# A fused attention and mixer kernel: the low-rank U product with x stationary, a turn by one matmul, other PSUM banks and a new order of the small steps

## The chip, the core and the metric

The kernel runs on one core of one Trainium2 chip. The metric is device time in microseconds (us) of one execution; several runs are taken and their median is given. TensorE does matrix products and writes them to PSUM, which has eight banks of 512 fp32 columns in each of 128 partitions. VectorE (DVE in the profile), ScalarE (ACT) and GpSimd (POOL) work on elements; SyncE (SP) issues DMAs. Each engine takes its instructions in the order in which the program gives them, and waits for others through semaphores.

## The reference

The inputs are q, k and v (batch 4, 8 heads, 768 positions, head width 64, fp32), and the mixer's U (768x32), V (32x768), w_ch1 (512x2048) and w_ch2 (2048x512). The output is 4x768x512 in fp32.

```python
def attn(q, k, v, n_global=8, n_local=96):
    scores = q @ k.transpose(0, 1, 3, 2) / sqrt(64)
    # keep: the first 8 positions, and the 96 positions up to and including the own one
    # bias: -slope[h] * distance (n_local for a far global position)
    a = softmax(where(keep, scores + bias, -1e9))
    return a @ v

def mixer(x, U, V, w_ch1, w_ch2):              # x: [batch, seq, 512], heads side by side
    h = x.transpose(0, 2, 1) @ U @ V           # mixes positions through rank 32
    u = x + h.transpose(0, 2, 1)
    return u + maximum(u @ w_ch1, 0) @ w_ch2
```

## The kernel before

**Attention.** Two heads make a pair, and the four batches of four pairs are 16 pairs, numbered `i`. Of the 768 positions, each block of 128 queries sees its own block of keys and the one before, in which 8 columns are replaced by the global keys (`kA`; `vA` for the values). The scores of one head are 1408 columns, made in three chunks `c` = 0, 1, 2 of 512, 512 and 384 columns. `s_pe` makes a chunk on TensorE (lines 361 and 366) in one of two `sc` banks, `s_dve` (line 392) adds the bias on DVE and empties the bank, `st_E` (line 404) takes one exponential over the 1408 columns on ACT. `st_V` (lines 416 and 420) multiplies by the values into the single `ob` bank; DVE takes a reciprocal (line 425) and scales into `x_sb` (line 433), POOL casts to fp16 (`x16`, line 434). Each matmul in `st_V` has 65 columns: 64 values and the sum of the softmax.

**Mixer, first part.** Once both heads of a pair are in `x16` (128 positions x 128 features for each of six blocks), the pair's slice of the low-rank product follows. `st_M1` multiplies U by x: six matmuls with U, padded from 32 to 128 columns, as the stationary operand and x as the moving one (line 442), summed in a bank; DVE copies the result, 128x128 with features along the columns, into `tmp16` (line 446). `st_M3` multiplies V by it, two halves of three matmuls (line 483), each half followed by an addition into `x_sb` on DVE (line 488); POOL casts the sum back to `x16` (line 491), and `st_X` transposes that by a DMA on SP's queue into `uT` (line 471). Batch 0 has another second half, `st_M2`, which the change doesn't touch.

**Mixer, second part.** `queue_ff` puts the large products of a batch's half into two queues: an "up" unit is four matmuls of 384 columns into a bank of the `th` kind (line 506), emptied by ACT with a ReLU into `htr` (line 510); a "down" unit is four matmuls of 512 columns into a `cps` bank (line 526), and after four of them DVE adds `x_sb` (line 532) and SP stores the result. `fill(n)` takes the next n units from these queues. It stands between the small steps, so that TensorE has something to do while other engines prepare the next step.

**PSUM.** Eight banks: two `sc`, one `ob`, two `cps` (down units and a few others) and three `th`. The `th` banks serve the up units, the transposes of q and k (`st_T`) and, before the change, the U product and both halves of `st_M3`.

**Order.** The program's order is written out by hand. After a first part for batch 0 (to about 33 us) a loop runs over `i` = 4 to 17; "step i" below is one turn of it. In step i the scores of pair i are made, the attention output of pair i-1 (`st_V`), and the low-rank product of pair i-1 (`st_M1`, `st_M3`, `st_X`). Pairs up to 7 get their transposes on TensorE (`st_T`), later ones by DMAs (`turn`, lines 324 and 327, on SP's queue), and then the key copies `st_K` (lines 340 and 341, on DVE) and the query copies `st_Z` (line 335, on POOL) prepare pair i+1 in step i. `cast_qk` (line 112) casts q and k of pair i+2 on POOL. `st_P` (line 311) is a small DVE copy into `vA` for pairs below 8. A step takes ten units (13 from step 9 on). Down units are held back until step 7, and in steps 9, 10 and 14 the queue gives up units for a while, as a new half begins there.

The tile `zw` is 128x512 in fp16, set to zero at the start and used only by the warm-up matmuls (`warm`, in the first 18 us).

Of the kernel before, what the change touches and what calls it, by code (L numbers as in the profile page):

```python
# [16 lines left out]
ALU = mybir.AluOpType  # L17
# [3 lines left out]
def kernel(  # L21
# [13 lines left out]
    nc = tc.nc  # L35
# [3 lines left out]
    P = 128  # L39
    DM = H * D  # L40
    NSB = S // P
# [3 lines left out]
    R = moe_U.shape[1]  # L45
    NP = H // 2
    NPE = 2 * NP
# [13 lines left out]
    GT = S // 2  # L61
    NTG = GT // P
# [11 lines left out]
    def ps_sc(tag="sc"):  # L74
        return psum.tile([P, 512], FP32, name="sc", tag=tag, bufs=2)

    def ps_ob():
        return psum.tile([P, 512], FP32, name="ob", tag="ob", bufs=1)
# [4 lines left out]
    def ps_th(name, dtype=FP32, cols=512):  # L83
        return psum.tile([P, cols], dtype, name=name, tag="th", bufs=3)
# [47 lines left out]
    NPAIR = B * NP  # L132
# [20 lines left out]
    zw = cst.tile([P, 512], FP16, name="zw")  # L153
# [27 lines left out]
    u16 = cst.tile([P, NSB, P], FP16, name="u16")  # L181
    v16w = cst.tile([P, S], FP16, name="v16w")
    for t in (qz[1][0][D:P], qz[1][1][0:D], u16.rearrange("p n c -> p (n c)"), v16w):
        nc.gpsimd.memset(t.bitcast(I32), 0)
    ident16 = cst.tile([P, P], FP16, name="ident16")
# [37 lines left out]
    w1v = moe_w_ch1.rearrange("(c p) n -> p c n", p=P)  # L223
    w2v = moe_w_ch2.rearrange("(c p) n -> p c n", p=P)

    def load_w1(c):
        js = slice(c * (DFF // 4), (c + 1) * (DFF // 4))
        nc.gpsimd.dma_start(w1_16[:, :, js], w1v[:, :, js])

    def load_w2(c):  # L230
        nc.gpsimd.dma_start(w2_16[:, 4 * c:4 * c + 4], w2v[:, 4 * c:4 * c + 4])


    xs, x16s, tmps, uTs = {}, {}, {}, {}

    def new_batch(b):
        xs[b] = xp.tile([P, NSB, DM], FP32, name="x_sb", tag="x_sb", bufs=3)
        x16s[b] = xp.tile([P, NP, NSB, P], FP16, name="x16", tag="x16")
        tmps[b] = xp.tile([P, DM], FP16, name="tmp16", tag="tmp16", bufs=3)
        uTs[b] = xp.tile([P, NDC, S], FP16, name="uT", tag="uT")  # L240
# [90 lines left out]
    def st_Z(i):  # L331
        tq = turned.pop(i).rearrange("d n p -> d (n p)")
        for hi in range(2):
            r = slice(hi * D, (hi + 1) * D)
            nc.gpsimd.tensor_copy(qz[i % 2][hi][r], tq[r])  # L335

    def st_K(i):
        kT = kts[i]
        kA = kp.tile([P, NSB - 1, P], FP16, name="kA", tag="kA")
        nc.vector.tensor_copy(kA.rearrange("d n p -> d (n p)"), kT[:, 0:S - P])  # L340
        nc.vector.tensor_copy(
            kA[:, 1:, 0:NG], kT[:, 0:NG].unsqueeze(1).broadcast_to((P, NSB - 2, NG))
        )
        kas[i] = kA
# [53 lines left out]
    def st_S(i, c):  # L398
        for hi in range(2):
            s_dve(i, hi, s_pe(i, hi, c))  # L400

    def st_E(i, hi):
        ep = scp.tile([P, W], FP16, name=f"ep{hi}", tag=f"ep{hi}")
        nc.scalar.activation(  # L404
            ep, sps.pop((i, hi)), AF.Exp, scale=slope[2 * (i % NP) + hi]
        )
        eps[i, hi] = ep
# [29 lines left out]
    def st_M1(i):  # L437
        b, dc = i // NP, i % NP
        ch = slice(dc * P, (dc + 1) * P)
        tps = ps_th("tmp_ps")  # L440
        for n in range(NSB):
            nc.tensor.matmul(  # L442
                tps[:, 0:P], u16[:, n], x16s[b][:, dc, n],
                start=(n == 0), stop=(n == NSB - 1),
            )
        nc.vector.tensor_copy(tmps[b][:, ch], tps[:, 0:P])

    def st_M2(i):
        b, dc = i // NP, i % NP
        ch = slice(dc * P, (dc + 1) * P)  # L450
        for g in range(2):
            ups = ps_th("ups")
            nc.tensor.matmul(
                ups[:, 0:GT], tmps[b][:, ch], v16w[:, g * GT:(g + 1) * GT],
                start=True, stop=False,
            )
            for t in range(NTG):
                nc.tensor.matmul(
                    ups[:, t * P:(t + 1) * P], x16s[b][:, dc, NTG * g + t], ident16,
                    start=False, stop=(t == NTG - 1),  # L460
                )
            dst = uTs[b][:, dc, g * GT:(g + 1) * GT]
            if dc < NP - 2 or (g == 0 and dc == NP - 1):
                nc.vector.tensor_copy(dst, ups[:, 0:GT])
            else:
                nc.scalar.copy(dst, ups[:, 0:GT])


    def st_X(i):
        b, dc = i // NP, i % NP  # L470
        nc.sync.dma_start_transpose(
            uTs[b][:, dc].rearrange("d (n p) -> d n p", n=NSB),
            x16s[b][:, dc].rearrange("p n d -> p (n d)"),
        )

    def st_M3(i):
        b, dc = i // NP, i % NP
        ch = slice(dc * P, (dc + 1) * P)
        for g in range(2):
            ups = ps_th("ups")  # L480
            for t in range(NTG):
                n = NTG * g + t
                nc.tensor.matmul(  # L483
                    ups[:, t * P:(t + 1) * P], v16w[:, n * P:(n + 1) * P], tmps[b][:, ch],
                    start=(t == 0), stop=(t == NTG - 1),
                )
            dst = xs[b][:, NTG * g:NTG * (g + 1), ch]
            nc.vector.tensor_tensor(  # L488
                dst, ups[:, 0:GT].rearrange("p (t d) -> p t d", t=NTG), dst, ALU.add
            )  # L490
        nc.gpsimd.tensor_copy(x16s[b][:, dc], xs[b][:, :, ch])  # L491

    ups_q, downs_q = deque(), deque()

# [70 lines left out]
    def fill(n):  # L565
        for _ in range(n):
            down = downs_q and not held[0] and not any(w == downs_q[0][1] for _, w in ups_q)
            room = ups_q and (not downs_q or downs_q[0][1] == ups_q[0][1]
                              or ups_q[0][1] in follows(downs_q[0][1]))
            if down and room:  # L570
                if ahead[0] > 0:
                    ahead[0] -= 4
                    downs_q.popleft()[0]()
                else:
                    ahead[0] += 3
                    ups_q.popleft()[0]()
            elif down:
                downs_q.popleft()[0]()
            elif room:
                ups_q.popleft()[0]()  # L580
            else:
                return

    def follows(w):
        b, g = w
        return ((b, 1),) if g == 0 else ((b + 1, 0),)
# [8 lines left out]
    for i in range(NP):  # L595
# [7 lines left out]
        if i == 2:  # L603
            load_w1(0)
        if i == 3:
            load_v(NP)
            load_w1(2)
        if i >= 2:
            st_M1(i - 2)
# [15 lines left out]
        if i == 2:  # L625
            load_w1(1)
# [19 lines left out]
    for i in range(NP, NPAIR + 2):  # L646
        b, hp = divmod(i, NP)
        live = i < NPAIR
        n = 1 if i < 2 * NP + 1 else 2
        held[0] = i < NP + 3  # L650
        if hp == 0 and live and b + 1 < B:
            new_batch(b + 1)
        if live and i > NP:
            st_S(i, 0)
        early = {NP: (NP + 2,), NP + 1: (NP + 3,), NP + 2: (NP + 5,)}
        for j in early.get(i, (i + 3,)):
            if j < NPAIR:
                load_qk(j)
        if i + 1 < NPAIR:
            load_v(i + 1)  # L660
        if i == NP + 1:
            load_qk(NP + 4)
        fill(2)
        if NP < i <= NPAIR:
            st_V(i - 1, 0)
        if i + 1 < NPE:
            st_T(i + 1)
        if live:
            cast_v(i)
            st_A(i)  # L670
            if i == NP + 1:
                load_w2(2)
        fill(n)
        if live:
            st_S(i, 1)
        fill(1)
        if NP < i <= NPAIR:
            st_V(i - 1, 1)
        if i == NP + 1:
            load_w2(3)  # L680
        if i > NP + 1 and (i - 2) % NP == NP - 1:
            queue_ff((i - 2) // NP, 0)
            queue_ff((i - 2) // NP, 1)
            ahead[0] = 1
        if i == NPAIR + 1:
            break
        fill(n)
        if live:
            st_S(i, 2)
            if i < NPE:  # L690
                st_P(i)
        if i + 1 < NPAIR:
            if i + 1 >= NPE:
                st_K(i + 1)
                st_Z(i + 1)
        if i + 2 < NPAIR:
            cast_qk(i + 2, nc.gpsimd)
        if i == NP:
            load_w2(0)
            load_w2(1)  # L700
        fill(1)
        if i > NP:
            st_M1(i - 1)
        if live:
            st_E(i, 0)
        fill(2)
        if i > NP:
            st_M3(i - 1)
            st_X(i - 1)
        if live:  # L710
            st_E(i, 1)
        if i + 2 < NPAIR and i + 2 >= NPE:
            turn(i + 2)
        fill(1 + n)
    while ups_q or downs_q:
        fill(1)
    ordered.close()
# [35 lines left out]
```

## Time and profile before

| | |
|---|---|
| median of 3 runs | 245.12 us (244.91 to 245.6) |
| the profiled execution's own time | 244.88 us |
| its span in the profile | 243.1 us |
| TensorE (PE) busy | 230.5 us, 95% |
| weight loads (PEld) | 141.4 us, 58% |
| DVE, ACT, POOL busy | 132.6, 118.8 and 93.8 us |
| line 442, U product | 96 matmuls of 128 columns, 16 of the groups of six |
| line 483, V product | 72 matmuls of 128 columns, 12 groups of six |

The profile is of one execution on the chip. An engine's busy time is the union of its instructions' spans. Matmuls are pipelined: the span of one (219 ns for 128 columns) is longer than the time after which the next can start (56 ns), so that TensorE reads as busy where it loses a little. The page gives shares of the span, a chain of waits followed back from the last instruction, and the groups of instructions by line. The timeline lists instructions with start, duration, engine and line, out<-in and a count; neighbours of one line are merged. A wait is given in brackets with the engine and line that ended it. Names as `hps<-uT,w` are the tiles written and read.

### The profile page before, as it was taken

To read this page: it belongs to the slowest core of one execution; us is meant where nothing else is said; L and a number is where in the kernel's file an instruction comes from. 1 tells how busy PE (TensorE), PEld (TensorE's weight loads), DVE (VectorE), ACT (ScalarE), POOL (GpSimd) and SP (SyncE) were. 2 spreads that over 40 slices of the span, in tenths; PEclk is the share of its full clock that TensorE was granted. 3 is DMA by queue.
4 is the path that set the end of the run, shared out by engine and by line. 5 is a ranking of instruction groups with operands and counts; after the bars stand their busy time and mean duration, and the time that the engine had idled before them with its cause. 6 is when DMAs were issued, how large, how long until landed. Compare 5 with 4: busy or idle time off the path is not lost.

```text
span 243.1 us, 4884 instructions
## 1 busy us (share of the span) xinstructions
PE 230.5 (95%) x1952; PEld 141.4 (58%) x1952; DVE 132.6 (55%) x273; ACT 118.8 (49%) x203; POOL 93.8 (39%) x141
## 2 busy tenths in 40 slices
PE   7898789989999999999999999999999999999994
PEld 2577666656565556675656555666565455555553
DVE  7768875868676967575757666755432111011121
ACT  5898568675832211866362507483733133543300
POOL 5479929475464535453545436332111000000000
PEclk9999999999999999999999999999999999999999
DMA  6999999999486979895958682812121201110022
GB/s 207 338 321 277 231 199 275 214 221 218 98 187 171 229 218 182 227 193 132 220 140 198 166 213 76 187 49 57 46 78 32 87 9 37 44 43 29 17 86 86
DMA packets 86558, 36.71 MB, mean 151 GB/s; under 512 B 74152, under 2 KB 83560, under 8 KB 86536
## 3 DMA queue, kind: packets, MB, share of 16 engines
q1 hardware_dynamic: 82312, 32.21, 52.4%
q0 software_dynamic: 4224, 4.19, 10.5%
q8 instruction: 15, 0.25, 0.4%
q14 instruction: 7, 0.06, 0.1%
HBM read 27.46 MB, written 6.29 MB: 139 GB/s over the span
## 4 chain that ended last, share of the span: by engine, by line
PE 75%; POOL 8%; ACT 6%; issue 4%; DVE 4%; POOLq 0%
PE cps L526 33%; PE hps L506 29%; ACT ep L404 3%; PE sc L361 3%; ACT htr L510 3%; PE sc L366 2%; PE ob L420 2%; PE tmp_ps L442 2%; POOL v L126 2%; PE ob L416 1%; PE cps L544 1%; POOL vA L298 1%; DVE sp L392 1%; POOL x L434 1%; POOL k L112 1%
## 5 line engine op out<-in xcount | busy, mean ns | idle before, releaser
L510 ACT ACTIVATE htr<-hps 128x384 f16<-128x384 f32 x128 | 61.7, 491 | 88.4 <-PE hps L506 87.3
L506 PE MATMUL hps<-uT,w 128*128 128x384 f16 x512 | 97.9, 326 | 1.2 <-ACT htr L510 0.5
L526 PE MATMUL cps<-w,htr 128*128 128x512 f16 x368 | 90.7, 379 | 0.0
L506 PEld LDWEIGHTS <-w 128*128 128x128 f16 x512 | 47.9, 98 | 32.5 <-issue 2.3
L392 DVE SCALAR_TENSOR_TENSOR sp<-sc,relcat 128x512 f32<-128x512 f32 (+1 forms) x72 | 43.1, 641 | 26.1 <-PE sc L366 21.5
L526 PEld LDWEIGHTS <-htr 128*128 128x128 f16 x368 | 34.6, 98 | 32.6
L532 DVE TENSOR_TENSOR osb<-cps,x_sb 128x512 f32<-128x512 f32 x23 | 15.9, 691 | 51.2 <-PE cps L526 50.9
L404 ACT ACTIVATE ep<-sp 128x1408 f16<-128x1408 f32 x24 | 32.7, 1372 | 12.4 <-DVE sp L392 12.4
L434 POOL CAST x<-x_sb 128x384 f16<-128x384 f32 x30 | 15.2, 510 | 59.8 <-DVE x_sb L433 59.8
L361 PE MATMUL sc<-qz,kT 128*128 128x128 f16 x192 | 27.6, 219 | 0.5 <-DVE sp L392 0.5
L366 PE MATMUL sc<-qz,kA 128*128 128x128 f16 x160 | 25.3, 219 | 0.3 <-DVE kA L285 0.3
L361 PEld LDWEIGHTS <-kT 128*128 128x128 f16 x192 | 18.3, 98 | 4.2 <-DVE kT L270 0.5
L366 PEld LDWEIGHTS <-kA 128*128 128x128 f16 x160 | 15.6, 98 | 6.9 <-issue 0.8
L491 POOL CAST x<-x_sb 128x768 f16<-128x768 f32 x12 | 9.9, 827 | 20.5 <-DVE x_sb L488 19.5
L433 DVE TENSOR_TENSOR x_sb<-ob,rcp 128x384 f32<-128x384 f32 x30 | 16.7, 558 | 1.0
L488 DVE TENSOR_TENSOR x_sb<-ups,x_sb 128x384 f32<-128x384 f32 x24 | 12.4, 553 | 7.7 <-PE ups L483 7.6
L420 PE MATMUL ob<-v,ep 128*128 128x65 f16 x192 | 15.8, 193 | 0.0
L126 POOL CAST v<-vst 128x768 f16<-128x768 f32 x16 | 13.8, 864 | 4.5 <-DMA vst<-in_v_dram 4.5
L420 PEld LDWEIGHTS <-ep 128*128 128x128 f16 x192 | 13.9, 98 | 2.1
L416 PE MATMUL ob<-vA,ep 128*128 128x65 f16 x160 | 14.0, 194 | 0.0
L335 POOL COPY qz<-qT 64x768 f16<-64x768 f16 x16 | 13.4, 834 | 0.5
L416 PEld LDWEIGHTS <-ep 128*128 128x128 f16 x160 | 10.9, 97 | 2.1
(79 smaller groups left out, 197.3 us busy)
## 6 DMA issues: line engine op xcount, KB each, us to landing
qst<-in_q_dram SPq DMA_DIRECT2D x16, 384.0 KB, 4.2
kst<-in_k_dram SPq DMA_DIRECT2D x16, 384.0 KB, 4.6
vst<-in_v_dram SPq DMA_DIRECT2D x16, 384.0 KB, 5.7
out_dram<-osb SPq DMA_DIRECT2D x23, 256.0 KB, 2.1
w<-in_moe_w_ch_dram POOLq DMA_DIRECT2D x8, 512.0 KB, 8.9
vA<-v SPq DMA_DIRECT2D x8, 152.3 KB, 3.6
out_dram<-osb SPq DMA_DIRECT2D x2, 128.0 KB, 1.7
uT<-x SPq DMA_TRANSPOSE x12, 2.8
```

Source lines behind the costliest of these rows:

```text
L126: nc.gpsimd.tensor_copy(vt.rearrange("p n h d -> p h n d")[:, :, :, 0:D], vsts.pop(i).rearrange("p (h n) d -> p h n d", h=2),)
L361: nc.tensor.matmul(sc[:, o:o + P], kT[:, kb * P:(kb + 1) * P], z[:, kb * P:(kb + 1) * P], start=(o == 0 and not on_pe), stop=(o + P == tot),)
L366: nc.tensor.matmul(sc[:, o + P:o + 2 * P], kA[:, kb], z[:, (kb + 1) * P:(kb + 2) * P], start=False, stop=(o + 2 * P == tot),)
L392: nc.vector.scalar_tensor_tensor(out=sps[i, hi][:, c0:c0 + tot], in0=sc[:, 0:tot], scalar=qk_scale / slope[2 * (i % NP) + hi], in1=relf[:, ...
L404: nc.scalar.activation(ep, sps.pop((i, hi)), AF.Exp, scale=slope[2 * (i % NP) + hi])
L416: nc.tensor.matmul(ob[:, qi], ep[:, OF[qi - 1]:OF[qi - 1] + P], vA[:, qi - 1, hi], start=True, stop=False,)
L420: nc.tensor.matmul(ob[:, qi], ep[:, DG[qi]:DG[qi] + P], vt[:, qi, hi], start=(qi == 0), stop=True,)
L433: nc.vector.tensor_tensor(xo, ob[:, :, 0:D], rb, ALU.mult)
L434: nc.gpsimd.tensor_copy(x16, xo)
L506: nc.tensor.matmul(hps[:, 0:GT], w1_16[:, dc, jt * P:(jt + 1) * P], uT[:, dc, ts], start=(dc == 0), stop=(dc == NDC - 1),)
L510: nc.scalar.activation(cell["htr"][:, jt], hps[:, 0:GT], AF.Relu)
L526: nc.tensor.matmul(cps, htr[:, jc, t * P:(t + 1) * P], w2_16[:, jc], start=(b > 0 and jc == 0), stop=(jc == NJC - 1),)
```

## The change

In the loop, that is for batches 1 to 3 (12 pairs), it does the following.

- `st_M1` makes the U product with x as the stationary operand and the 32 real columns of U as the moving one: six matmuls of 32 columns instead of 128. The result has features along the partitions, so it must be turned. DVE copies its 32 columns into one of two quarters of `zw` (`turn16`; the other 96 columns there stay zero), and a new step, `st_MT`, multiplies that by an identity (one matmul of 128 columns) and copies the result into `tmp16`.
- Banks: the U product, its turn and the second half of `st_M3` use the `ob` bank of the attention output, the first half of `st_M3` an `sc` bank of the scores. None of them uses `th` any more.
- Order: before, a step ended with one unit, U product, exponential of head 0, two units, both halves of `st_M3` and `st_X`, exponential of head 1, and 1+n units (n is 1, from step 9 on 2). Now it is: one unit, U product, exponential of head 0, one unit, turn, one unit, first half, exponential of head 1, one unit, second half and `st_X`, and the rest. In steps 4 to 6 one unit moves from the end of the step to the place ahead of score chunk 2. The number of units of a step stays.
- `st_K` goes from its place ahead of the U product to the place after the turn; `st_Z` keeps its place on POOL's queue.

```diff
--- before.py
+++ after.py
@@ -223,6 +223,8 @@
     w1v = moe_w_ch1.rearrange("(c p) n -> p c n", p=P)
     w2v = moe_w_ch2.rearrange("(c p) n -> p c n", p=P)
 
+    turn16 = [zw[:, i * P:(i + 1) * P] for i in range(2)]
+
     def load_w1(c):
         js = slice(c * (DFF // 4), (c + 1) * (DFF // 4))
         nc.gpsimd.dma_start(w1_16[:, :, js], w1v[:, :, js])
@@ -437,6 +439,15 @@
     def st_M1(i):
         b, dc = i // NP, i % NP
         ch = slice(dc * P, (dc + 1) * P)
+        if b:
+            tps = ps_ob()
+            for n in range(NSB):
+                nc.tensor.matmul(
+                    tps[:, 0:R], x16s[b][:, dc, n], u16[:, n, 0:R],
+                    start=(n == 0), stop=(n == NSB - 1),
+                )
+            nc.vector.tensor_copy(turn16[i % 2][:, 0:R], tps[:, 0:R])
+            return
         tps = ps_th("tmp_ps")
         for n in range(NSB):
             nc.tensor.matmul(
@@ -444,6 +455,12 @@
                 start=(n == 0), stop=(n == NSB - 1),
             )
         nc.vector.tensor_copy(tmps[b][:, ch], tps[:, 0:P])
+
+    def st_MT(i):
+        b, dc = i // NP, i % NP
+        tps = ps_ob()
+        nc.tensor.matmul(tps[:, 0:P], turn16[i % 2], ident16, start=True, stop=True)
+        nc.vector.tensor_copy(tmps[b][:, dc * P:(dc + 1) * P], tps[:, 0:P])
 
     def st_M2(i):
         b, dc = i // NP, i % NP
@@ -473,22 +490,22 @@
             x16s[b][:, dc].rearrange("p n d -> p (n d)"),
         )
 
-    def st_M3(i):
+    def st_M3(i, g):
         b, dc = i // NP, i % NP
         ch = slice(dc * P, (dc + 1) * P)
-        for g in range(2):
-            ups = ps_th("ups")
-            for t in range(NTG):
-                n = NTG * g + t
-                nc.tensor.matmul(
-                    ups[:, t * P:(t + 1) * P], v16w[:, n * P:(n + 1) * P], tmps[b][:, ch],
-                    start=(t == 0), stop=(t == NTG - 1),
-                )
-            dst = xs[b][:, NTG * g:NTG * (g + 1), ch]
-            nc.vector.tensor_tensor(
-                dst, ups[:, 0:GT].rearrange("p (t d) -> p t d", t=NTG), dst, ALU.add
+        ups = ps_ob() if g else ps_sc()
+        for t in range(NTG):
+            n = NTG * g + t
+            nc.tensor.matmul(
+                ups[:, t * P:(t + 1) * P], v16w[:, n * P:(n + 1) * P], tmps[b][:, ch],
+                start=(t == 0), stop=(t == NTG - 1),
             )
-        nc.gpsimd.tensor_copy(x16s[b][:, dc], xs[b][:, :, ch])
+        dst = xs[b][:, NTG * g:NTG * (g + 1), ch]
+        nc.vector.tensor_tensor(
+            dst, ups[:, 0:GT].rearrange("p (t d) -> p t d", t=NTG), dst, ALU.add
+        )
+        if g == 1:
+            nc.gpsimd.tensor_copy(x16s[b][:, dc], xs[b][:, :, ch])
 
     ups_q, downs_q = deque(), deque()
 
@@ -684,34 +701,41 @@
             ahead[0] = 1
         if i == NPAIR + 1:
             break
-        fill(n)
+        more = 1 if i + 1 < NPE else 0
+        fill(n + more)
         if live:
             st_S(i, 2)
             if i < NPE:
                 st_P(i)
-        if i + 1 < NPAIR:
-            if i + 1 >= NPE:
-                st_K(i + 1)
-                st_Z(i + 1)
+        fill(1)
+        if i > NP:
+            st_M1(i - 1)
+        if NPE <= i + 1 < NPAIR:
+            st_Z(i + 1)
         if i + 2 < NPAIR:
             cast_qk(i + 2, nc.gpsimd)
         if i == NP:
             load_w2(0)
             load_w2(1)
+        if live:
+            st_E(i, 0)
         fill(1)
         if i > NP:
-            st_M1(i - 1)
-        if live:
-            st_E(i, 0)
-        fill(2)
+            st_MT(i - 1)
+        if NPE <= i + 1 < NPAIR:
+            st_K(i + 1)
+        fill(1)
         if i > NP:
-            st_M3(i - 1)
-            st_X(i - 1)
+            st_M3(i - 1, 0)
         if live:
             st_E(i, 1)
+        fill(1)
+        if i > NP:
+            st_M3(i - 1, 1)
+            st_X(i - 1)
         if i + 2 < NPAIR and i + 2 >= NPE:
             turn(i + 2)
-        fill(1 + n)
+        fill(n - more)
     while ups_q or downs_q:
         fill(1)
     ordered.close()
```

## The prediction, made before the changed kernel was built or run

> **What bounds the kernel now.** I read the page first, then the waits, then the timeline of single steps.
>
> ```profile
> PE 230.5 (95%) x1952; PEld 141.4 (58%) x1952; DVE 132.6 (55%) x273; ACT 118.8 (49%) x203; POOL 93.8 (39%) x141
> ...
> PEclk9999999999999999999999999999999999999999
> ...
> PE 75%; POOL 8%; ACT 6%; issue 4%; DVE 4%; POOLq 0%
> ```
>
> TensorE is busy 95% at the full granted clock and holds 75% of the chain: it is the bound, and a microsecond counts only if it is TensorE's. POOL's 8% lies in the first 33 us, which the change leaves alone. The 95% hides waits, since a matmul row is longer than its share of the pipeline. So I take spacings between starts: eight 384-column matmuls from 50.24 to 51.55 are 163 ns apart, 512 columns 216, 128 columns 56, 65 columns 30 (11 in 0.33 us). Whatever a group starts after "previous start + count x spacing" is lost. Summed over the trace this gives 16.4 us, 9.4 before 33 us and 7.0 after. Those 7.0 are what can be won beside matmul time. The waits name some of them:
>
> ```profile
> PE tmp_ps L442 <- POOL x L434: 1.8, 3, 1.2
> PE tmp_ps L442 <- ACT htr L510: 0.5, 1, 0.5
> PE ups L483 <- DVE tmp L446: 0.5, 2, 0.3
> PE sc L361 <- DVE sp L392: 0.5, 2, 0.3
> PE hps L506 <- ACT htr L510: 0.5, 2, 0.3
> ```
>
> By place: step 4 (33 to 44.6 us) 1.2, step 5 1.8, step 6 1.5, steps 9, 10 and 14 0.8 each, all other steps under 0.1. In the steps without loss "down" units lie between the small products; in the six with loss nearly all units are "up" units, each needing an eviction by ACT. Step 9 shows how it comes about:
>
> ```profile
> 95.83 0.81 PE L506 MATMUL hps<-uT,w 128*128 128x384 f16 x4
> 96.47 0.50 PE L442 MATMUL tmp_ps<-x,u 128*128 128x128 f16 x6
> ...
> 96.80 0.70 DVE L340 COPY kA<-kT 128x640 f16<-128x640 f16 x1
> 96.81 1.46 PE L506 MATMUL hps<-uT,w 128*128 128x384 f16 x8
> 97.06 1.37 ACT L404 ACTIVATE ep<-sp 128x1408 f16<-128x1408 f32 x1
> ...
> 97.54 0.70 DVE L341 COPY kA<-kT 128x32 f16<-128x32 f16 x1
> 98.15 0.28 DVE L446 CAST tmp<-tmp_ps 128x128 f16<-128x128 f32 x1
> 98.33 0.86 ACT L510 ACTIVATE htr<-hps 128x384 f16<-128x384 f32 x2
> 98.48 0.71 PE L483 MATMUL ups<-tmp,v16w 128*128 128x128 f16 x6 [0.20 <-DVE tmp L446]
> ```
>
> The U product is done at 96.81, but its copy (L446) stands on DVE behind the two key copies (96.80 to 98.15) and ends at 98.43, so L483 starts 0.37 late. Then its second bank and the next up unit wait 0.22 each for ACT, which was in a 1.37 us exponential: L442, L483 and the up units share the three `th` banks. Sum 0.8. Step 5 is different:
>
> ```profile
> 48.56 0.81 PE L506 MATMUL hps<-uT,w 128*128 128x384 f16 x4
> 49.91 0.50 PE L442 MATMUL tmp_ps<-x,u 128*128 128x128 f16 x6 [0.54 <-ACT htr L510]
> 50.24 1.46 PE L506 MATMUL hps<-uT,w 128*128 128x384 f16 x8
> 51.55 0.50 PE L483 MATMUL ups<-tmp,v16w 128*128 128x128 f16 x6
> 52.29 1.14 PE L506 MATMUL hps<-uT,w 128*128 128x384 f16 x6 [0.24 <-ACT htr L510]
> ```
>
> L442 is due at 49.21 and starts at 49.91, 0.70 late (POOL's cast of its operand ends at 49.86); the up unit after L483 is 0.41 late; score chunk 2 had lost 0.51 at 47.80 and 48.40, waiting for DVE to empty the `sc` banks.
>
> **Part by part.** *The matmuls.* Per unit, now 6 x 56 = 0.33 us; then six with 32 columns and one turn of 56 ns. No row has 32 columns. Nearest is the 65-column row, which also loads 128 weights for each matmul:
>
> ```profile
> 102.94 0.10 PEld L416 LDWEIGHTS <-ep 128*128 128x128 f16 x1
> 102.97 0.10 PEld L420 LDWEIGHTS <-ep 128*128 128x128 f16 x1
> ```
>
> Loads of 98 ns start every 30 ns, so they overlap. Upper bound 56 ns (no gain, the turn extra: +0.06 x 12 = +0.7 us); lower bound 16 ns, the line through 128 and 65 columns carried on (6 x 40 - 56 = 0.18, x 12 = -2.2 us). I take 30, since fewer columns cannot be slower than 65 with equal loads, and nothing shows loads closer: 6 x 26 - 56 = 0.10, x 12 = **-1.2 us**.
>
> A page speaks against this term: the Trainium skill, "TensorE: Matmul & The Clock Gate", section "LDWEIGHTS (loading the stationary operand)", has a load cost its columns over 1.2 GHz, 107 ns for 128, whatever the moving side. If loads set the pace, six would stay six, the turn would add a seventh, and the sum would be some 1.3 us worse than nothing. The 30 ns between loads above disagrees, and the measurement decides.
>
> *Key copies behind the turn, banks, steps a unit apart (steps 9, 10, 14).* I walk step 9 with the same rows. Chunk 2's two DVE passes end at 96.88; the copy of 32 columns takes 0.2 to 0.28 (reciprocal of 6 columns 0.19, L446 0.28), so it is back at 97.15. TensorE: U product 96.47 to 96.65, up unit to 97.30, so the turn finds it ready, cover 0.15. The turn's copy ends about 97.85; after one more up unit M3's first half starts on time at 98.0. The key copies follow, 97.85 to 99.2; the next scores need them at 100.3, cover 1.1. Behind them waits the first M3 addition (to 99.75); the second head's score bank needs that at 100.5. With M3 out of `th`, the up units reach a used bank three units later, after 98.82 and 99.19, when ACT has freed them; one late start of 0.13 stays at 100.75. So 0.8 less 0.13 is **0.66 per step, 2.0 for three**. If the cover of 0.15 were gone, each 0.1 of it costs 0.1 per step.
>
> *Steps 4 to 6, one unit moved ahead of chunk 2.* In step 4 the exponentials start 0.65 later, as ACT takes the moved unit's eviction first; 0.72 of late starts go, but the transposes then wait 0.39 for a `th` bank: 0.3 won. In step 5 the moved unit covers the 0.51 at chunk 2. The U product still waits for POOL, whose queue holds a key copy, v casts and a weight DMA issue (48.61 to 49.35), until 49.6: 0.6 late instead of 0.7, with that extra unit already done. Then DVE has two score passes and the 0.76 copy L311 ahead of the 32-column copy: the turn is 0.2 late. M3 and the next up units are on time. 0.7 won. In step 6 the same walk leaves 0.15 (kT copy) + 0.35 (POOL) + 0.37 (turn) = 0.87 of 1.5, 0.65 won. Sum **-1.7 us**. Bounds: 0, if ACT only hands its waits on, to -4.1 if all late starts but the untouched 0.42 at 36.50 vanish.
>
> *Elsewhere* (7, 8, 11 to 13, 15, 16): between U product and turn lies a unit of 0.65 to 1.08 us, and DVE answers about 0.5 us after chunk 2's passes. Cost nothing; without the cover 0.2 to 0.4 per step.
>
> *Queues.* POOL keeps its order (L335 then L112); only its M3 cast (L491) comes a unit later, hence L471 about 0.45 us later on SP, and behind it the next transposes, loads and the vA copies. These were issued by 98.48 and take 3.6 to land, so about 102.1, for a use at 102.94, which moves up to about 102.2: just covered. In step 16 the last L471 would land near 189.2, used from 191.2.
>
> **Sum.** -1.2 - 2.0 - 1.7 = -4.9. The profiled execution took 244.88 us (span 243.1 and 1.8 around it): 240.0. The median of the three runs is 0.24 above it, so **240.2**.
>
> **Rivals.** *Slower: the single `ob` bank becomes a relay.* Each unit now crosses DVE twice (copy, turn's copy) before M3, and everything behind the turn on TensorE stops until DVE answers. In step 9 of today the answer took 1.62 us (96.81 to 98.43). At that length a 0.65 us unit leaves 0.97 open, 12 x 0.97 = 11.6 us. It decides once the mean wait per unit exceeds 4.9/12 = 0.41 us, an answer over 1.06 us. At a middling 0.6 per unit: +7.2 - 4.9, 247.4 us. For: L311 and output additions (0.69) can stand ahead; DVE is 75% busy from 68 to 80 us. Against: the key copies that made up most of the 1.62 are now behind.
>
> *Faster, but ACT and POOL keep steps 4 to 6, or vA comes late.* The first leaves -1.2 - 2.0: 241.9; the second costs up to 0.4 in three steps: 241.4; with 32 columns at 56 ns as well, 243.8.
>
> *Better: every wait goes.* 7.0 - 0.42 + 1.2 = 7.8: 237.3.
>
> *The banks don't bind*, so that nothing but matmul time changes, and the turn eats that: 245.1.
>
> **Numbers.** Forecast 0.60, better 0.10, partial 0.17, no difference 0.03, slower 0.10. Faster, by over the 0.3% (0.7 us) that a measurement of this kernel can tell from none: 0.87; within: 0.03; slower: 0.10. The range runs from 237.3 (better) to 243.0, into the partial cases; slower, no difference and the worst partial mix, some 0.17, stay outside.
>
> **What would show it.** Right: 32-column matmuls about 30 ns apart; no late start at M3 and its next up unit in steps 9, 10 and 14; the sum of late starts after 33 us near 3.3 instead of 7.0; score chunk 2 of steps 5 and 6 without its 0.43. Wrong: turns or second M3 halves that start late for DVE in most steps, spacing near 56 ns, or attention output (L416) waiting for a vA landing.

## The result: 239.74 us after 245.01, and the profile after

The changed kernel takes 239.74 us (median of 4 runs, 239.29 to 240.05); the kernel before, beside it on the same chip, 245.01. The ratio is 0.978, with a 95% interval of 0.9766 to 0.9793. The forecast was 240.2, in a range from 237.3 to 243.0. The profiled execution took 239.92 us, its span is 238.0.

Line numbers shift a little: 445 is the U product now, 449 its copy into `zw`, 462 the turn, 463 the copy into `tmp16`, 499 the V product, 504 its addition, 508 the cast behind it, 523 and 527 an up unit and its eviction, 342 and 343 the key copies. From the page of the changed kernel, its engines, the granted clock and the chain:

```profile
PE 227.5 (96%) x1964; PEld 139.8 (59%) x1964; DVE 134.1 (56%) x285; ACT 117.9 (50%) x203; POOL 93.8 (39%) x141
...
PEclk9999999999999999999999999999999999999999
...
PE 78%; POOL 8%; DVE 6%; DMA 2%; ACT 2%; issue 2%; SPq 1%; POOLq 0%
```

TensorE is still the bound and holds 78% of the chain; ACT's share of the chain fell from 6% to 2%. Twelve matmuls more are in the program (1964), one turn for each of twelve pairs, and as many DVE copies (285 against 273). The waits of the changed kernel that answer to those shown of before:

```profile
PEld L445 <- POOL x L436: 1.3, 2, 0.8
...
PEld L462 <- DVE zw L449: 0.9, 3, 0.4
...
PE ob L445 <- POOL x L436: 0.4, 1, 0.4
...
PE sc L499 <- DVE tmp L463: 0.3, 1, 0.3
PE hps L523 <- ACT qz L291: 0.3, 1, 0.3
...
PE tp L257 <- ACT htr L527: 0.2, 1, 0.2
```

No V product waits for ACT any more. One up unit of step 4 still starts 0.42 late, at 36.84, for ACT's copy of the transposed queries (L291), as it did in the kernel before; the other late starts of up units are 0.17 at most (steps 9 and 14). The U product waits for POOL as before; the wait now shows at the weight loads too, since x is the stationary operand. New are the turn's wait for `zw` and a wait of the transposes for a `th` bank. Step 9, the example of the prediction, in the timeline of the changed kernel:

```profile
93.54 0.81 PE L523 MATMUL hps<-uT,w 128*128 128x384 f16 x4
...
94.19 0.30 PE L445 MATMUL ob<-u,x 128*128 128x32 f16 x6
...
94.34 0.81 PE L523 MATMUL hps<-uT,w 128*128 128x384 f16 x4
...
94.53 0.19 DVE L449 CAST zw<-ob 128x32 f16<-128x32 f32 x1
94.77 1.37 ACT L406 ACTIVATE ep<-sp 128x1408 f16<-128x1408 f32 x1
...
94.99 0.22 PE L462 MATMUL ob<-ident,zw 128*128 128x128 f16 x1
...
95.24 0.29 DVE L463 CAST tmp<-ob 128x128 f16<-128x128 f32 x1 [0.52 <-PE ob L462]
95.45 0.70 DVE L342 COPY kA<-kT 128x640 f16<-128x640 f16 x1
...
95.69 0.33 PE L499 MATMUL sc<-tmp,v16w 128*128 128x128 f16 x3
```

The six matmuls start at 94.19, and the next unit at 94.34: 25 ns each. The copy into `zw` ends at 94.72, well ahead of the turn at 94.99, which starts when it is due (94.34 + 4 x 162 ns). The copy into `tmp16` ends at 95.53, the first half starts on time at 95.69, and the key copies run behind.

Late starts, counted as in the prediction, after 33 us: 3.1 us against 7.0. By step: 4 to 6 together 2.3 against 4.5; step 9 0.17, step 10 none, step 14 0.17, against 0.8 each; step 15 0.44 against none.

One number for all that follows: the program up to the first up unit (about 33 us) is alike in all these kernels, and yet its length differs from execution to execution (32.6 to 33.8 us). So I also give the *loop*: the span less the start of the first up unit. Before it is 243.1 - 33.0 = 210.1 us, after 238.0 - 33.3 = 204.7, and in a second profile of the changed kernel 238.5 - 33.8 = 204.7 again. The change is worth 5.4 us in the loop.

### The profile page after: what moved, and what is told of

Its sections match the earlier page's. It is cut to its first block, busy times and chain, and to the rows that moved or that the text cites. A ratio compares the mean times of both kernels' runs of the same rounds, so it can differ in the third digit from the quotient of the medians.

```text
span 238.0 us, 4937 instructions
## 1 busy us (share of the span) xinstructions
PE 227.5 (96%) x1964; PEld 139.8 (59%) x1964; DVE 134.1 (56%) x285; ACT 117.9 (50%) x203; POOL 93.8 (39%) x141
## 4 chain that ended last, share of the span: by engine, by line
PE 78%; POOL 8%; DVE 6%; DMA 2%; ACT 2%; issue 2%; SPq 1%; POOLq 0%
PE cps L543 33%; PE hps L523 31%; PE sc L363 3%; PE sc L368 2%; DMA vst<-in_v_dram 2%; PE ob L422 2%; POOL x L436 2%; PE cps L561 1%; PE ob L418 1%; POOL v L126 1%; POOL vA L300 1%; ACT ep L406 1%; POOL w L230 1%; PE sc L499 1%; PE ob L445 1%
## 5 line engine op out<-in xcount | busy, mean ns | idle before, releaser
L523 PEld LDWEIGHTS <-w 128*128 128x128 f16 x512 | 47.0, 98 | 29.2 <-issue 0.4
L543 PEld LDWEIGHTS <-htr 128*128 128x128 f16 x368 | 34.1, 98 | 31.2
L112 POOL CAST k<-kst 128x768 f16<-128x768 f32 x14 | 12.1, 867 | 0.1
```

Of the source, the lines that this page charges most:

```text
L523: nc.tensor.matmul(hps[:, 0:GT], w1_16[:, dc, jt * P:(jt + 1) * P], uT[:, dc, ts], start=(dc == 0), stop=(dc == NDC - 1),)
L543: nc.tensor.matmul(cps, htr[:, jc, t * P:(t + 1) * P], w2_16[:, jc], start=(b > 0 and jc == 0), stop=(jc == NJC - 1),)
```

## The experiments

The theory: TensorE is the bound; the parts win matmul time (form of the product), waits for `th` banks (banks), waits for DVE (key copies behind the turn) and waits of steps 4 to 6 (the moved unit). The rivals: a part does nothing, or the new trip over DVE costs more than it saves. One part was not taken out by itself: the small steps of the product standing a unit apart.

### Key copies ahead of the product again

```diff
             if i < NPE:
                 st_P(i)
+        if NPE <= i + 1 < NPAIR:
+            st_K(i + 1)
         fill(1)
...
             st_MT(i - 1)
-        if NPE <= i + 1 < NPAIR:
-            st_K(i + 1)
```

> The changed kernel with the key copies put back ahead of the U product. Theory (the new relay over DVE is short only because the key copies stand behind it): in steps 7 to 14 the copy into zw waits for the two key copies (0.5 to 1.4 us of DVE), the turn is late by about 1.1 us in steps 9, 10 and 14, where a unit of 0.65 us covers it, and by 0.2 to 0.7 in the other five, where a unit of 0.86 does: 3 to 6 us slower than the changed kernel, so 243 to 246. Rival (the place of the key copies only moved an idle wait, the units cover DVE anyway): within 0.5 us of the changed kernel's 239.7.

Measured: 245.45 us, ratio to the kernel before 1.0004 (0.9990 to 1.0018); loop 210.5, 5.8 longer than the changed kernel's. The whole gain is gone. Step 9 in its timeline:

```profile
95.08 0.81 PE L523 MATMUL hps<-uT,w 128*128 128x384 f16 x4
...
95.25 0.63 DVE L342 COPY kA<-kT 128x640 f16<-128x640 f16 x1
...
95.92 0.70 DVE L343 COPY kA<-kT 128x32 f16<-128x32 f16 x1
96.53 0.18 DVE L449 CAST zw<-ob 128x32 f16<-128x32 f32 x1
...
96.77 0.23 PE L462 MATMUL ob<-ident,zw 128*128 128x128 f16 x1 [0.87 <-DVE zw L449]
```

The turn is due at 95.08 + 0.65 = 95.73 and starts at 96.77, 1.03 late, behind both key copies. In the eight steps 7 to 14 it is late by 0.85, 0.46, 1.03, 0.70, 0.77, 0.76, 0.76 and 0.67, in sum 6.0. The whole is as expected, the split is not: 0.70 and 0.67 in steps 10 and 14, where I had expected 1.1, and 0.46 to 0.85 in the other five, where I had expected 0.2 to 0.7. This is the relay of the prediction's rival. In step 9 it costs nearly what the rival named (0.97); over the program it costs 6.0, in eight steps, against the rival's 11.6, or 7.2 at its middling length, in twelve. It is the place of the key copies that keeps it away.

### The key copies alone, on the kernel before

`st_K` goes behind the U product's copy (L446); all else as before.

> The kernel before with one part alone: the key copies behind the copy of the U product (L446). Theory (two waits stand one behind the other): the first half of the V product in steps 9 and 10 starts 0.37 and 0.45 us earlier, but its second half and the next up unit wait for the same th banks that ACT frees behind the exponential, so nothing is won: within 0.3 us of the kernel before. Rival (the wait that the profile names, DVE's L446, is the binding one): 0.8 us faster.

Measured: 244.97 us, ratio 0.9995 (0.9983 to 1.0007); loop 210.1, the same. Step 9 of it (old line numbers):

```profile
96.60 1.46 PE L506 MATMUL hps<-uT,w 128*128 128x384 f16 x8
...
97.90 0.33 PE L483 MATMUL ups<-tmp,v16w 128*128 128x128 f16 x3
...
98.12 0.86 ACT L510 ACTIVATE htr<-hps 128x384 f16<-128x384 f32 x2
...
98.65 0.33 PE L483 MATMUL ups<-tmp,v16w 128*128 128x128 f16 x3 [0.42 <-ACT htr L510]
```

The first half is on time (96.60 + 8 x 162 ns = 97.90): the wait for DVE that the profile named is gone. The second half is 0.59 late instead, for a `th` bank that ACT empties behind its exponential, the next up unit 0.22: 0.8 together, as before. The named wait stood in front of another that ended just as late.

### The banks alone, on the kernel before

```diff
-        tps = ps_th("tmp_ps")
+        tps = ps_ob() if b else ps_th("tmp_ps")
...
-            ups = ps_th("ups")
+            ups = ps_ob() if g else ps_sc()
```

> The kernel before with one part alone: for batches 1 to 3 the U product and the second half of the V product in the ob bank, the first half in an sc bank. Theory: the waits for th banks go, 0.43 us each in steps 9 and 10, 0.8 in step 14, 0.4 each in steps 5 and 6, while the waits for DVE behind the key copies and for POOL stay: 2.0 to 2.6 us faster than the kernel before. Rival (the single ob bank is the new bottleneck): no gain, or slower.

Measured: 242.44 us, ratio 0.9898 (0.9875 to 0.9922), 2.6 us faster; loop 207.2, 2.9 less. Step 9 of it (old line numbers):

```profile
97.66 0.28 DVE L446 CAST tmp<-ob 128x128 f16<-128x128 f32 x1
...
97.99 0.33 PE L483 MATMUL sc<-tmp,v16w 128*128 128x128 f16 x3 [0.23 <-DVE tmp L446]
...
98.16 0.33 PE L483 MATMUL ob<-tmp,v16w 128*128 128x128 f16 x3
```

The first half is still 0.39 late for DVE, but the second half follows it at once. Late starts after 33 us are 4.1: beside these 0.39, steps 10 and 14 keep no more than 0.04, and steps 5 and 6 lost their 0.41 each. In step 10, where I had expected the wait for DVE to stay, the key copies took 0.32 and 0.68, and the product's copy came in time. Of the two parts tried alone, this is the one that works.

### The banks back to th, in the changed kernel

The U product, turn and both halves take `ps_th` again.

> The changed kernel with the U product, the turn and both halves of the V product back in the three th banks; order and matmuls as in the changed kernel. Theory (ACT's 1.37 us exponentials reach TensorE through the shared th banks): in steps 9, 10 and 14 the first half waits for the up unit after the exponential, about 0.8 to 0.9 us each, and steps 5 and 6 lose 0.4 to 0.9 each; steps with down units lose nothing: 3 to 4.5 us slower than the changed kernel, 243 to 244.5. Rival (the banks were never short once the order is spread out): within 0.5 us of 239.7.

Measured: 242.77 us, ratio 0.9904 (0.9890 to 0.9919); loop 207.8, 3.1 longer than the changed kernel's. The size is at the low end of what I expected; in step 9 the place is nearly right:

```profile
96.50 0.33 PE L499 MATMUL ups<-tmp,v16w 128*128 128x128 f16 x3
...
96.85 0.86 ACT L527 ACTIVATE htr<-hps 128x384 f16<-128x384 f32 x2
...
97.39 0.81 PE L523 MATMUL hps<-uT,w 128*128 128x384 f16 x4 [0.55 <-ACT htr L527]
```

In step 9 the first half is on time, and the up unit behind it, due at 96.67, starts at 97.39. I had put the wait at the first half itself; it came one group later. Steps 9, 10 and 14 lose 1.1, 1.0 and 0.9 us. Steps 5 and 6 lose only 0.07 and 0.23 more than in the changed kernel, where I had expected 0.4 to 0.9 each; the steps with down units lose 0.1 at most.

### Without the moved unit

```diff
-        more = 1 if i + 1 < NPE else 0
+        more = 0
```

> The changed kernel without the unit that moved ahead of score chunk 2 in steps 4 to 6. Theory (the unit fills waits of chunk 2 for DVE and of the U product for POOL): 0.65 us lost in step 5, about 0.45 in step 6 (there the turn's wait of 0.2 goes), 0.3 in step 4: 1.3 to 1.5 us slower, 241.0 to 241.3. Rival (the other banks alone freed steps 4 to 6): within 0.3 us of 239.7.

Measured: 241.91 us, ratio 0.9858 (0.9841 to 0.9875); loop 206.4, 1.7 longer. Score chunk 2 waits 0.43 for DVE again in steps 5 and 6, the U product 0.70 and 0.46 for POOL (0.56 and 0.31 with the moved unit), and step 4 has its 0.44 and 0.28 again. The direction is as expected, the size in the loop 0.2 to 0.4 above; the medians, which have the first 33 us in them, lie 2.2 apart.

### The old form of the product, in the changed kernel

U stationary again, 128 columns of x moving, the result copied straight to `tmp16`; no turn.

> The changed kernel with the U product in its old form (U stationary, x moving, 128 columns, copied straight to tmp16, no turn), in the new banks and places. Theory (the form pays in TensorE time alone: 6 x 56 against 6 x 25 + 56 ns, 0.13 us per pair, 1.56 for 12, while the turn's own waits of 0.07, 0.20 and 0.44 us in steps 5, 6 and 15 go): 0.8 to 1.5 us slower, 240.5 to 241.2. Rival (the form is a loss, its extra DVE trip costs more than the matmuls save): 0.3 us or more faster than 239.7.

Measured: 240.33 us, ratio 0.9792 (0.9777 to 0.9808), an interval that overlaps the changed kernel's, and a median just below the 240.5 to 241.2 expected. By the time alone, what the form is worth can't be told from nothing; the rival, that it costs more than it saves, is not supported. The profile is clearer: the loop is 205.8, 1.1 longer. Matmul starts take 1.56 us more, and late starts after 33 us are 2.7 against 3.1. The turn's waits go, but in the waits of this kernel a new one stands:

```profile
PEld L418 <- DMA vA<-v: 0.7, 2, 0.4
```

In steps 9 and 10 the attention output was 0.19 and 0.35 late for the `vA` copies on SP's queue: the cover that the prediction called "just" enough.

### All 128 columns moving, with x stationary

> The changed kernel with all 128 columns of the padded U moving instead of 32; only the width of the 72 matmuls changes, the results used are the same. Theory (start to start goes with the columns, 56 against 25 ns): 72 x 31 ns = 2.2 us slower, 241.9. Rival (the weight loads set the pace of these six, so width is free): within 0.3 us of 239.7.

Measured: 241.13 us, ratio 0.9848 (0.9827 to 0.9870); loop 206.4, 1.7 longer. The width is not free, so weight loads don't set the pace of these six at 128 columns: they start every 56 ns, against 25 with 32. Of the 2.2 us that this makes, 0.5 came back as fewer late starts (2.6 against 3.1): the turns of steps 5 and 6, coming later, no longer wait for DVE (0.27), and the up units of steps 9 and 14 start on time (0.34), while one attention output is 0.08 late.

### One more unit ahead of the product

In steps 5 and 6 a unit moves from between the halves of the V product to ahead of the U product; the exponential of head 0 goes ahead of that unit and head 1's behind the turn; `st_P` goes behind the U product's copy in steps 5 to 7.

> The changed kernel with the waits that are left in steps 5 and 6 covered: one more unit ahead of the U product (taken from between the two halves of the V product), the exponentials keeping two units between them, and the DVE copy of st_P behind the U product's copy in steps 5 to 7. Theory (the late starts of 0.56 + 0.07 in step 5 and 0.31 + 0.20 in step 6 go): 0.9 to 1.1 us faster than the changed kernel, 238.6 to 238.8. Rival (the units taken away uncover a wait for ACT or for tmp16 of the same size): within 0.3 us of 239.7.

Measured: 239.91 us, ratio 0.9788 (0.9773 to 0.9804); loop 204.8. Nothing won; the rival held. Step 5 into step 6 of this kernel:

```profile
51.84 0.56 DVE L504 TENSOR_TENSOR x_sb<-sc,x_sb 128x384 f32<-128x384 f32 x1 [0.49 <-POOL k L112]
...
52.45 0.22 PE L363 MATMUL sc<-qz,kT 128*128 128x128 f16 x1 [0.33 <-DVE x_sb L504]
```

The U product is on time now, but the next step's second score chunk (52.45) waits for the `sc` bank of the V product's first half, which DVE empties at 52.40: 0.49 late in each of the two steps. The first half is 0.25 and 0.03 late as well. The unit that stood between the halves had given DVE the time.

### The same, with the V product in cps banks

The edit of `late_u`, and one more: no down unit runs in steps 5 and 6, so the `cps` banks are free there. `st_P` now goes behind the turn's copy. The changed kernel ran once more beside it.

```diff
-        ups = ps_ob() if g else ps_sc()
+        if i + 1 < NPE - 1:
+            ups = ps_cps("ups")
+        else:
+            ups = ps_ob() if g else ps_sc()
```

> The changed kernel once more, beside the two that follow: 239.7 again, every theory alike.

> The kernel of late_u, with both halves of the V product in cps banks in steps 5 and 6 (no down unit runs there) and st_P behind the turn's copy. Theory (what late_u lost again, 0.49 us in each of the two steps, was the next step's second score bank waiting for the addition of the first half, and 0.25 the turn's copy behind st_P): the late starts of steps 5 and 6 fall from 1.1 us in the changed kernel to about 0.1 beside the transposes' waits, so 0.9 to 1.1 us faster than the changed kernel, 238.6 to 238.8. Rival (DVE or ACT is simply full in these steps, and the wait moves on once more): within 0.3 us of the changed kernel.

Measured: 239.86 us for the changed kernel (ratio 0.9781, 0.9754 to 0.9808) and 238.69 for this one (0.974, 0.971 to 0.977); loops 204.7 and 203.6. In its profile steps 5 and 6 keep 0.14 and 0.07 behind the kT copies, and the U product, the turn, the V product and the scores start on time. 1.1 us as expected, which the loops show; the intervals still overlap.

### Transposes in cps banks too, and step 15 mended

> The kernel of late_u_cps, and the transposes of q and k of steps 4 to 6 in cps banks as well, and in step 15 the first half of the V product one unit later. Theory: the waits of up units and transposes for th banks go (0.42 at 36.8, 0.38 at 44.2, 0.07 and 0.14 behind the kT copies), and the 0.44 in step 15 behind the output addition: 1.3 to 1.5 us more than late_u_cps, 237.2 to 237.5. Rival (ACT sets the pace of steps 4 to 6, the wait comes back at the next up unit): only the 0.44 of step 15, 238.2.

> The same kernel as all_cps, since its six times spread from 237.7 to 240.3. Theory (the waits in the loop are gone, and the spread comes from the first 33 us, whose late starts went from 9.0 to 9.8 between kernels that are alike there): the profiled span less its late starts before 33 us is again about 226.0, against 227.2 for late_u_cps and 228.8 for the changed kernel; median 237.5 to 238.5. Rival (a wait that comes only in some executions lies in the loop, as banks are shared more): the median stays near 239.3, and a slow profile shows late starts after 33 us of over 1.5.

Measured: 239.33 us (0.9755, 0.9724 to 0.9786; 237.74 to 240.31) and when run again 239.14 (0.9750, 0.9734 to 0.9765). Neither reaches the 237.2 to 237.5 expected, and neither median is below the 238.69 of `late_u_cps`. The two profiles differ: loop 202.4 with 0.8 us of late starts after 33 us, and loop 204.2 with 2.6. In both, the waits in question are gone, and a new one of 0.4 stands at score chunk 2 of step 5. The rival of the second expectation holds: another wait comes in some executions. In the second profile the U product of step 7 is 1.35 late:

```profile
66.82 0.84 POOL L126 CAST v<-vst 128x768 f16<-128x768 f32 x1 [2.00 <-DMA vst<-in_v_dram]
...
67.72 0.73 POOL L301 COPY vA<-v 128x650 f16<-128x650 f16 x1
...
68.40 0.51 POOL L437 CAST x<-x_sb 128x384 f16<-128x384 f32 x1
...
68.96 0.32 PE L446 MATMUL ob<-u,x 128*128 128x32 f16 x6 [1.19 <-POOL x L437]
```

POOL waits 2.0 us for a load of v, and the cast that the U product needs stands behind it. The issue of that load began on SP's queue at 60.85 and took 2.75; in the first profile it began at 59.24 and took 1.43. Ahead of it a transposing DMA's issue held the queue from 53.25 for 5.89 us; in the first profile that took 1.31, and a load of k behind it 3.68. A long hold does not make the wait by itself: in the second profile of the changed kernel the same transposing DMA held the queue for 4.15 us, and nothing in step 7 was late. So in this execution a load set the pace of step 7; why the transposing DMA was held so long was not tried.

## Why the prediction was right

**Matmul time.** Forecast -1.2 us with 30 ns per matmul of 32 columns; they start 25 ns apart, and the sum of all starts fell from 221.5 to 219.9, by 1.56 us. The term was 0.36 too small, within its bounds of 16 and 56 ns. The same page of the Trainium skill ("TensorE: Matmul & The Clock Gate", section "Wait — 56ns, not 53.3ns?") says that starts never come closer than about 25 ns, however few the columns; of the 72 matmuls here none came closer (median 25, least 25, widest 39). The section on weight loads that the prediction weighed, 107 ns each, does not hold as a pace for such a run of loads: a load's row lasts 96 ns on average, and the matmuls, each with its own load, start 25 apart.

**Steps 9, 10 and 14.** Forecast -2.0. Late starts fell from 2.4 to 0.35. The walk holds by line: the copy into `zw` came 0.27 ahead of the turn (0.15 forecast), and the up unit behind the next scores kept 0.17 (0.13). But the parts do not share this as the prediction's heading has them, side by side. `before_banks` alone leaves 0.43 of the 2.4, so the banks give nearly all of it; `before_k` leaves it all, since the waits stood one behind the other. The place of the key copies is what the new trip over DVE asks for, as `k_ahead` shows. What the small steps gain by standing a unit apart was not tried by itself.

**Steps 4 to 6.** Forecast -1.7; late starts fell by 2.2 in the profile taken with the result, 1.7 longer loop without the moved unit. The single waits: transposes 0.38 (0.39 forecast), U product 0.56 and 0.31 (0.6 and 0.35), kT copy 0.07 and 0.14 (none named, and 0.15). The turns' waits, 0.07 and 0.20, were overrated (0.2 and 0.37), in part because DVE's copy from 32 columns takes 0.17 there, not up to 0.28. Of the 0.5 between 1.7 and 2.2, a part is arithmetic: the prediction's own terms for step 5 (0.51 at chunk 2, 0.1 at the U product, 0.41 at the up unit, less 0.2 at the turn) make 0.8, not the 0.7 that it adds up.

**Elsewhere.** "Cost nothing" failed at one step. In step 15 of the changed kernel, as the timeline has it:

```profile
166.70 0.81 PE L523 MATMUL hps<-uT,w 128*128 128x384 f16 x4
166.84 0.69 DVE L549 TENSOR_TENSOR osb<-cps,x_sb 128x512 f32<-128x512 f32 x1 [0.68 <-PE cps L543]
...
167.45 0.28 DVE L463 CAST tmp<-ob 128x128 f16<-128x128 f32 x1
...
167.79 0.33 PE L499 MATMUL sc<-tmp,v16w 128*128 128x128 f16 x3 [0.27 <-DVE tmp L463]
```

A down unit ended just ahead of the turn, so its output addition stands on DVE before the turn's copy, and the V product is 0.44 late. The prediction named such an addition in the slower rival, but gave it no price in this step: its look at these steps ends at the turn.

**The sum.** -4.9 forecast; the loop is 5.4 shorter (1.56 of matmul time and 3.9 of late starts), and the first 33 us of this execution were 0.3 longer, so 244.88 became 239.92. That this falls within 0.1 of the 240.0 forecast for it is in part luck, since the change does not touch the first 33 us. That the total of late starts came to 3.1 where 3.3 was forecast is partly two errors against each other: 0.5 too little for steps 4 to 6, 0.44 forgotten in step 15.

**The rivals.** The relay is real, but only with the key copies in its way (6.0 us). It is a wait for what DVE copies rather than for the one bank: with the `th` banks back (`banks_th`) the turns of steps 5 and 6 and the V product of step 15 are late by the same 0.07, 0.20 and 0.44. Of the partial cases, `vA` was in time here and late in `old_form`, as the thin cover said; in the second profile of `all_cps` it was late too, by 0.43 in step 10.

## What to carry to other kernels

A wait that a profile names is worth removing only as far as the next one behind it lets go: walk the step with the wait taken out before pricing it, bank by bank. When a step gains a trip over another engine, put what is long on that engine's queue behind the trip, and count every instruction that can end up ahead of each copy, those of the filler work too. To measure parts of a few tenths of a per cent, take a stretch that the change alone can move (here the loop), since the loads at the start of the kernel differ by more than a part is worth.

## What was not expected of the hardware

The small key copy on DVE (128x32) takes 0.68 to 0.70 us while POOL runs a copy or cast, and 0.18 when POOL is idle: in the kernel before at 159.57, in the changed one at 155.54. Of its sixteen executions in the two profiles, the other fourteen ran beside POOL and took the long time. Step 9 of the changed kernel:

```profile
95.92 0.92 POOL L112 CAST k<-kst 128x768 f16<-128x768 f32 x1
...
96.18 0.68 DVE L343 COPY kA<-kT 128x32 f16<-128x32 f16 x1
```

The cast ends at 96.84 and the copy at 96.86. So it is in all fourteen: the copy ends 0.03 us after the POOL instruction that was running when it began. Its length is what POOL had left to do; what holds it was not tried. In `late_u`, where `st_P`'s DVE copy of 8 partitions ran beside a cast of POOL's, it took 1.06 us and ended 0.16 after the cast, against 0.28 at the least in the kernel before. POOL being busy is not enough: a copy of that kind took 0.30 in the kernel before at 71.80, where POOL's instruction ended 0.16 after it began.
